# A new written order for the first half of a two-block attention kernel: 761 letters of TensorE work and 96 projections

## The chip, the cores and the metric

One core of one Trainium2 chip. The metric is the device time of one execution in microseconds (us), the median of several runs; less is better.

## What is computed

Two blocks of multi-head attention on their own inputs, their results side by side. Both have 2048 tokens, width 512 and 32 heads of 16. Block A looks back over a window of 256 tokens, block B at every token.

```python
qkv = (x @ wqkv).reshape(B, S, 3, H, Dh)          # both blocks, then q, k, v per head
scores = einsum("bhqd,bhkd->bhqk", q, k) * (Dh ** -0.5)
...
mask = (idx[:, None] - idx[None, :] >= 0) & (idx[:, None] - idx[None, :] < W)   # block A alone, W = 256
scores = where(mask, scores, -1e9)
...
p = softmax(scores)
out = einsum("bhqk,bhkd->bhqd", p, v) ... @ wo
return concatenate([a, b], axis=-1)
```

## The kernel before, in words

The program has two parts, one after the other on TensorE (PE). The first part does all of block A but its last projection, and also the projections to q, k and v of block B. The second part does block B by short cyclic patterns (line 45 on) and the output projections. The change touches the first part only.

The heads are in groups of four (g = 0 to 7), the queries in chunks of 512 (c = 0 to 3). A group and a chunk make a **unit**; each block has 32. Products of q, k and v go through HBM: a projection's result is copied out of PSUM, stored (`parts`, `vd`), and read back as the tiles `oq` (queries of one unit, 4 buffers), `opk` (keys of one group, 2 buffers) and `vt` (values).

The order of TensorE's work in the first part is written out by hand as a string, `ORDER_A`, one letter to a step:

- `p`: one projection on the whole array, 12 matmuls of 128 rows (line 309). Which one it is, the list `ORDER_P` says (`Aq02` is block A, queries, head pair 0, chunk 2; `Av13` is values, chunk 1, tile 3).
- `g`: a quarter of two projections that run side by side on two halves of the array's rows (line 444, 12 matmuls). Four `g` make two entries of `ORDER_P`.
- `m`: scores of one pair of heads for their maximum (line 607 for block A, line 561 for block B's first units); VectorE masks and reduces them (lines 616 and 617, or 612 and 564). It takes two neighbouring PSUM banks. Line 607's matmuls also use two halves of the rows. `e` is the same for block B's very first unit.
- `t`: the maxima of a unit are transposed (line 681), copied by ScalarE (683) and sent to the query tile by DMA (688).
- `s`: the scores again, of two heads, with the maximum as extra rows (line 717, two halves of the rows, two banks), then the exponential on ScalarE (line 724) and the mask on GpSimd (line 735).
- `w`: the exponentials times the values (line 764, matmuls on 32 columns of the array).

In the text below a projection is `p` or `g`, a maximum `m`, a score `s`, a weighing `w`, a transposition `t`. They use the array in three shapes: whole (`p`), halves of the rows (`g`, `m`, `e`, `s`) and columns (`w`, `t`).

While the program is being written, a planner (`Model`, line 90) keeps a clock for every engine and goes through the string (line 1122). It decides where between the letters DMAs are issued and copies are placed, and which PSUM banks a step gets; line 95 holds its charges for a change of shape. Loads of queries stand in a list of their own and come when the unit three before has its scores done:

```python
self.mode, self.turn = "f", dict(f=210, h=200, c=139)                 # line 95
...
list_("q", lambda u=u: done["s"] >= u - 3, stored(b, g // 2, 0, (c,)), load_q_at, b, g, c)   # line 1088
...
x = "p" if gen[0] else todo_a[0]                                      # line 1130
```

All DMAs are issued by SyncE's queue (SP), in one order. Everything is in order on its engine.

Of the kernel before, what the change touches and what calls it, by code (L numbers as in the profile page):

```python
# [57 lines left out]
FILL = 16  # L58
WARM = 22
ORDER_P = (  # L60
# [4 lines left out]
    "Bq20 Bq12 Bk30 Bk31 Bk10 Bq33 Bq30 Bq31 Bk32 Bq32 Bk33 Bk21 ").split()  # L65
WAKE = 200
GAP_V = 1500
PIECE = 4
# [4 lines left out]


ORDER_A = (
    "pppppppppppmmmmpmmgmgmptmgmgmmpmsgmsgmmpmsgmsgmwtsmgmsgmmpmsgsmgmtwwmmmpsmgmsgmswwmsgmsgmmpmssptwsmg"
    "msgmswsmgsmgmmwwmgmsgmstwmsgmsgmmwtsgmsgmswmsgmsgmswmmmpssmtwwmspmsmwssmgsmgmswtmsgsmgmwsmswssmwmmmp"
    "mtmswmsswmsmpsmmpsmwtmmmpsmswmmspmsmwsmsmwwtmsmsmsmpmsmtwsmsmwsmmswssmwmmspmmswsmwtsmgmsgmswsmgsmtgm"
    "mwsmwsmmswsmsmpsmmwmswtmsmwsmmmpmsssmmwsmsmwtmmmpsmswmsmsmwtsmsmwsmmpmmswsmtwmmmpmsgmsgmswtsmgmswpsm"
    "gsmwwmsgmmgmpmsgmsgsmwwtsmgmsgmswsmgsmgmmwtsgsmgsmwwmsgmsgmgsmgmswsmgmmgmwsmwtmsgmsgmswtmsgsmgmswwsm"  # L80
    "gmsgmswsmgsmgsmtwwmmmpmsmpmsmwsmmswtmsgmsgmswsmgsmgsmwmsmtwsmmswssmwmmmpmssmtwswmmmpmsgsmgsmwwmsgsmg"
    "etwmmmpmsgmsgmswsegsmgegesgmswsmgesgemtwmmpmsmwmswmsgsmgestwmsgesgmmpemmpmsmwwtemmpsmgmsgsmwmgegsewm"
    "mmpesstwmgmsgeswsmgsmgsmwesgsmgsmwmgsmgmswesmpsmmwtwmmmpmmmwp")
LAND = 400
LAND_V = 0
LGAP = 2500
# [1296 lines left out]
```

## Time and profile before

| | before |
|---|---|
| runs: median (lowest to highest) of 3 | 1776.33 us (1774.88 to 1779.42) |
| the profiled execution's own time | 1775.89 us |
| its span, first to last instruction | 1774.2 us |
| PE busy | 1756.8 us, 99% of the span |
| VectorE (DVE) busy | 1527.2 us, 86% |
| ScalarE (ACT) busy | 1402.2 us, 79% |
| GpSimd (POOL) busy | 648.5 us, 37% |
| granted TensorE clock | 1.000 of full speed |

The profile is of one execution. The time of an engine's instructions against the span is its share; PE's matmuls overlap and their ends are modelled, so that 99% does not say that PE never waits. The difference of the starts of two steps that follow each other on PE says what the first of them cost, its waiting and the wait of the next one included.

### The profile page before, as it was taken

To read this page: it belongs to the slowest core of one execution; us is meant where nothing else is said; L and a number is where in the kernel's file an instruction comes from. 1 tells how busy PE (TensorE), PEld (TensorE's weight loads), DVE (VectorE), ACT (ScalarE), POOL (GpSimd) and SP (SyncE) were. 2 spreads that over 40 slices of the span, in tenths; PEclk is the share of its full clock that TensorE was granted. 3 is DMA by queue.
4 is the path that set the end of the run, shared out by engine and by line. 5 is a ranking of instruction groups with operands and counts; after the bars stand their busy time and mean duration, and the time that the engine had idled before them with its cause. 6 is when DMAs were issued, how large, how long until landed. Compare 5 with 4: busy or idle time off the path is not lost.

```text
span 1774.2 us, 38875 instructions
## 1 busy us (share of the span) xinstructions
PE 1756.8 (99%) x14774; PEld 912.2 (51%) x14774; DVE 1527.2 (86%) x2386; ACT 1402.2 (79%) x2749; POOL 648.5 (37%) x1334
## 2 busy tenths in 40 slices
PE   8999999999999999999999999999999999999999
PEld 6776657767754444444444444444444444444456
DVE  4766786676779999999999999999999999999921
ACT  4466676665569888888889999999999999899894
POOL 0377888655755441222201123231112322121420
PEclk9999999999999999999999999999999999999999
DMA  8865667645663224111310311120031131010012
GB/s 267 200 210 199 206 206 223 177 146 163 201 181 108 66 86 89 41 41 41 83 37 17 77 29 30 47 62 17 17 78 35 30 65 38 17 38 26 20 44 102
DMA packets 129354, 166.78 MB, mean 94 GB/s; under 512 B 23204, under 2 KB 59044, under 8 KB 129156
## 3 DMA queue, kind: packets, MB, share of 16 engines
q1 hardware_dynamic: 129168, 164.31, 31.8%
q8 instruction: 116, 1.90, 0.5%
q14 instruction: 70, 0.57, 0.1%
HBM read 94.49 MB, written 68.19 MB: 92 GB/s over the span
## 4 chain that ended last, share of the span: by engine, by line
PE 89%; DVE 4%; DMA 2%; ACT 1%; SPq 1%; issue 1%; POOL 1%; POOLq 0%; ACTq 0%; DVEq 0%
PE ps_all L749 28%; PE ps_all L717 19%; PE ps_all L561 18%; PE ps_all L444 11%; PE ps_all L309 6%; PE ps_all L764 4%; DVE mt L564 3%; PE ps_all L607 3%; ACT p L724 1%; DMA in<-xT_A 1%; DVE nm L617 1%; PE ps_all L681 0%; SPq L473 0%; DVE ps_all L616 0%; DMA parts<-st 0%
## 5 line engine op out<-in xcount | busy, mean ns | idle before, releaser
L724 ACT ACTIVATE p<-ps_all 128x512 f32<-128x512 f32 x2432 | 1262.9, 598 | 204.8 <-PE ps_all L717 137.6
L564 DVE TENSOR_REDUCE mt<-ps_all 128x1 f32<-128x512 f32 (+1 forms) x1658 | 1212.7, 808 | 33.1 <-PE ps_all L561 28.0
L717 PE MATMUL ps_all<-oq,opk 51*128 51x512 f32 (+2 forms) x2752 | 756.9, 401 | 4.0 <-ACT p L724 2.0
L561 PE MATMUL ps_all<-opk,oq 48*128 48x512 f32 x2016 | 661.2, 435 | 0.2
L749 PE MATMUL ps_all<-p,vt 128*17 128x512 f32 (+1 forms) x5488 | 571.0, 490 | 0.0
L717 PEld LDWEIGHTS ps_all<-oq,opk 51*128 51x128 f32 x2752 | 385.8, 185 | 219.2 <-ACT p L724 142.7
L561 PEld LDWEIGHTS ps_all<-opk,oq 48*128 48x128 f32 x2016 | 304.6, 184 | 273.4 <-DVE mt L564 164.7
L735 POOL TENSOR_SCALAR_AFFINE_SELECT p<-p 128x256 f32<-128x256 f32 x480 | 179.0, 408 | 110.0 <-ACT p L724 107.4
L749 PEld LDWEIGHTS ps_all<-p,vt 128*17 128x17 f32 x5488 | 93.6, 95 | 214.2 <-issue 201.4
L616 DVE COPY_PREDICATED ps_all<-mone,ps_all 128x256 f32<-128x256 uint16 x224 | 95.3, 425 | 82.6 <-PE ps_all L607 75.9
L617 DVE TENSOR_REDUCE nm<-ps_all 128x2 f32<-128x512 f32 x224 | 155.2, 693 | 7.7
L633 POOL TENSOR_TENSOR mu<-mt 128x16 f32<-128x16 f32 x31 | 6.9, 222 | 409.9 <-DVE mt L564 409.9
L635 POOL TENSOR_TENSOR mu<-mt,mm 128x16 f32<-128x16 f32 x62 | 13.6, 220 | 388.7 <-DVE mt L564 388.7
L444 PE MATMUL ps_all<-x,w 64*128 64x512 f32 x720 | 119.2, 392 | 0.0
L444 PE MATMUL ps_all<-w_o,x_o 64*128 64x512 f32 x576 | 110.2, 394 | 0.0
L309 PE MATMUL ps_all<-x,w 128*128 128x512 f32 x408 | 102.7, 400 | 2.4 <-ACT x L257 1.7
L764 PE MATMUL ps_all<-p,vt 128*17 128x384 f32 (+2 forms) x1408 | 94.1, 386 | 0.1
L607 PE MATMUL ps_all<-opk,oq 48*128 48x384 f32 (+2 forms) x512 | 92.1, 361 | 2.0 <-DMA oq<-parts 0.5
L803 POOL TENSOR_TENSOR rd<-ld,minus 128x32 f32<-128x32 f32 x15 | 81.9, 5459 | 19.6 <-DMA ld<-od 19.6
L444 PEld LDWEIGHTS ps_all<-x,w 64*128 64x128 f32 x720 | 84.4, 185 | 8.9
L309 PEld LDWEIGHTS ps_all<-x,w 128*128 128x128 f32 x408 | 74.2, 188 | 24.8 <-ACT p L724 2.9
L392 ACT ACTIVATE raw<-ps_all 128x512 f32<-128x512 f32 x56 | 32.2, 596 | 68.5 <-PE ps_all L309 53.6
(79 smaller groups left out, 1042.7 us busy)
## 6 DMA issues: line engine op xcount, KB each, us to landing
parts<-st SPq DMA_DIRECT2D x64, 512.0 KB
oq<-parts SPq DMA_DIRECT2D x128, 128.0 KB
opk<-parts SPq DMA_DIRECT2D x128, 128.0 KB
od<-ou SPq DMA_DIRECT2D x64, 256.0 KB
vd<-vst SPq DMA_DIRECT2D x32, 272.0 KB
oq<-parts SPq DMA_DIRECT2D x128, 64.0 KB
opk<-parts SPq DMA_DIRECT2D x128, 64.0 KB
t<-od SPq DMA_DIRECT2D x32, 256.0 KB
```

The costliest lines, as they stand in the source:

```text
L309: nc.tensor.matmul(ps, l(u), r(v), start=start and k == 0, stop=stop and k == n - 1)
L444: op = nc.tensor.matmul(ps[a ^ turn], l(u)[rows], r(v)[rows], start=turn == q == 0, stop=turn == 1 and q == 11)
L561: nc.tensor.matmul(ps[:, a - lo], q[rows, 128 * qt:128 * qt + 128], k[rows, kc * QC:kc * QC + QC], start=True, stop=True)
L564: op = nc.vector.tensor_reduce(out=m[:, kc, lo:lo + len(sides), r, qt], in_=ps, axis=AX.X, op=ALU.max)
L607: nc.tensor.matmul(two[:, a, 0:w], opq[b, g, c][rows, r, 128 * qt:128 * qt + 128], opk2(g)[rows, r, t0:t1], start=True, stop=True)
L616: nc.vector.copy_predicated(two[:, :, 256:384], later, two[:, :, 0:128])
L617: op = nc.vector.tensor_reduce(out=m[:, :, r, qt, 0], in_=two[:, :, 128:384], axis=AX.X, op=ALU.max)
L717: nc.tensor.matmul(ps[x][:, col:col + n1], opk2(g)[rows, pr, 128 * k:128 * k + 128], opq[b, g, c][rows, pr, q0:q0 + n1], start=True, stop= ...
L724: op = nc.scalar.activation(p[:, a0 + x, :w], ps[x][:, :w], AF.Exp, scale=SCALE)
L735: nc.gpsimd.affine_select(out=v, in_=v, pattern=[[0, 2], [sign, 128]], compare_op=ALU.is_ge, fill=zero_fill, base=base, channel_multiplier ...
L749: nc.tensor.matmul(o[32 * j:32 * j + VW, q0:q1], vt[(g // 2) % 2][:, kt, vc:vc + VW], pts[1, g, c, kt, j // 2][:, j % 2, q0:q1], start=kt ...
L764: nc.tensor.matmul(o[32 * j:32 * j + VW, q0:q0 + w], vt[(g // 2) % 2][:, kt, vc:vc + VW], pts[b, g, c, m, j // 2][:, j % 2, col:col + w], ...
```

## The change

Only the two tables are new. The letters are the same in number (48 `p`, 96 `g`, 280 `m`, 16 `e`, 33 `t`, 192 `s`, 96 `w`), and so are the 96 entries of `ORDER_P`; their order is another from the fourth entry and the eleventh letter on. The planner's code and its charges stay as they were, and the second part of the program stays instruction by instruction.

```diff
 ORDER_P = (
-    "Aq00 Ak00 Ak01 Av11 Av02 Av03 Aq01 Av01 Ak02 Av21 Av13 Aq02 Av12 Av00 Aq03 Ak03 Av20 Av10 Av33 Ak20 Av32 "
...
+    "Aq00 Ak00 Ak01 Av03 Av02 Av11 Aq01 Aq02 Av00 Av23 Av10 Ak02 Av13 Av01 Aq03 Ak03 Av33 Av21 Av30 Av31 Ak10 "
...
 ORDER_A = (
-    "pppppppppppmmmmpmmgmgmptmgmgmmpmsgmsgmmpmsgmsgmwtsmgmsgmmpmsgsmgmtwwmmmpsmgmsgmswwmsgmsgmmpmssptwsmg"
...
-    "mtmswmsswmsmpsmmpsmwtmmmpsmswmmspmsmwsmsmwwtmsmsmsmpmsmtwsmsmwsmmswssmwmmspmmswsmwtsmgmsgmswsmgsmtgm"
...
+    "ppppppppppmmpmmpmmggmmpmgtmgmmpmsgmsgmmpmsgmsgmtwmmgsgmmpmsgmsgmtswwmmmpmsgssgswmsgmmptwmsgmmpsmswsm"
...
+    "ptmswmsswmmmpmmsptmsmwmmmpmsswmmspmsmwtsmsmwmsmswsmmpmtmswmswsmsmmswmmswssmmpmsmwwtmsgmsgsswmgsmgmst"
...
```

Counted over the whole strings, neighbours change like this (before, after): `s` then `m` 94, 37; `m` then `s` 97, 131; `s` then `g` 46, 72; `s` then `w` 32, 54; `w` then `m` 32, 55; `w` then `s` 31, 21; `m` then `w` 37, 17; `m` then `m` 59, 69; `m` then `g` 46, 18; `g` then `m` 59, 75. Changes of the array's shape (before, after): rows to columns 84, 92; columns to rows 84, 96; rows to whole 35, 38; whole to rows 35, 34; whole to columns 2, 4; columns to whole 2, 0. In sum 242 and 264.

Three places of which the prediction speaks. The first is ScalarE's queue in the first 45 us. `st` and `vst` are copies of projections out of PSUM (queries and keys; values), `x_3` is the splitting of the input's last chunk.

```order
 L388 ACTIVATE st_0_0_1_321<-ps_all 128x512
-L508 ACTIVATE vst_80<-ps_all 128x32x16
+L388 ACTIVATE st_0_0_2_337<-ps_all 128x512
 L257 ACTIVATE x_3_0_343<-in_3_0_288 128x512
 L257 ACTIVATE x_3_1_346<-in_3_0_288 128x512
-L257 ACTIVATE x_3_2_357<-in_3_2_290 128x512
-L257 ACTIVATE x_3_3_360<-in_3_2_290 128x512
-L388 ACTIVATE st_0_1_2_363<-ps_all 128x512
+L257 ACTIVATE x_3_2_358<-in_3_2_290 128x512
+L257 ACTIVATE x_3_3_361<-in_3_2_290 128x512
+L508 ACTIVATE vst_80<-ps_all 128x32x16
```

Before, the copy of the keys of chunk 2 (`st_0_1_2`) is the first thing after the splitting, and that of a value tile stands ahead of it; now the copy of the queries of chunk 2 (`st_0_0_2`) stands ahead of it, and the value tile's behind.

The second place is PE at the first use of the queries of unit (3,0), that is group 3, chunk 0 (`oq_3_0`), before:

```order
L717 MATMUL ps_all<-oq_2_1_1854,opk_75 128x256 x4
L607 MATMUL ps_all<-opk_75,oq_2_3_2210 128x384 x2
L717 MATMUL ps_all<-oq_2_1_1854,opk_75 128x384 x2
L717 MATMUL ps_all<-oq_2_1_1854,opk_75 128x128 x2
L607 MATMUL ps_all<-opk_75,oq_2_3_2210 128x384 x2
L309 MATMUL ps_all<-x_2_0_239,w_3_0_1298 128x512 x3
L309 MATMUL ps_all<-x_2_1_242,w_3_0_1298 128x512 x3
L309 MATMUL ps_all<-x_2_2_252,w_3_0_1298 128x512 x3
L309 MATMUL ps_all<-x_2_3_255,w_3_0_1298 128x512 x3
L607 MATMUL ps_all<-opk_76,oq_3_0_2450 128x128 x2
```

and now:

```order
L717 MATMUL ps_all<-oq_2_1_1991,opk_75 128x256 x4
L764 MATMUL ps_all<-p_2_0_2_0_2415,vt_78 17x256 x2
L764 MATMUL ps_all<-p_2_0_2_1_2448,vt_78 17x256 x2
L717 MATMUL ps_all<-oq_2_1_1991,opk_75 128x384 x2
L717 MATMUL ps_all<-oq_2_1_1991,opk_75 128x128 x2
L607 MATMUL ps_all<-opk_75,oq_2_3_2192 128x384 x2
L607 MATMUL ps_all<-opk_76,oq_3_0_2453 128x128 x2
L309 MATMUL ps_all<-x_1_0_168,w_3_0_1276 128x512 x3
L309 MATMUL ps_all<-x_1_1_171,w_3_0_1276 128x512 x3
L309 MATMUL ps_all<-x_1_2_189,w_3_0_1276 128x512 x3
L309 MATMUL ps_all<-x_1_3_192,w_3_0_1276 128x512 x3
```

A whole projection stood ahead of the first use of `oq_3_0` and now stands behind it. Between the last score that reads the buffer before (`oq_2_0`) and this first use there were 17 letters, `mwsmsmwwtmsmsmsmp`; now there are 15, `mwtsmsmwmsmswsm`. For unit (3,1) the letters between were `mtwsmsmwsmmswssmwm`, and are `wmswsmsmmswm`.

The third place is SP's queue ahead of the load of the same tile, before:

```order
L782 DMA od_0_3_1614<-ou_1_3_2391 128x512
L525 DMA vt_77<-vd_261 128x4x136
L411 DMA parts_2_1_935<-st_2_1_1_2294 128x2x512
L525 DMA vt_77<-vd_261 128x4x136 x2
L272 DMA in_1_0_2435<-xT_B 128x512
L796 DMA ld_0_3_2441<-od_0_3_1614 128x1x32
L489 DMA oq_3_0_2450<-parts_1_0_1411 16x2x512
```

and now:

```order
L782 DMA od_0_3_1617<-ou_1_3_2396 128x512
L525 DMA vt_77<-vd_261 128x4x136 x3
L796 DMA ld_0_3_2443<-od_0_3_1617 128x1x32
L411 DMA parts_2_1_2093<-st_2_1_2_2367 128x2x512
L489 DMA oq_3_0_2453<-parts_1_0_1164 16x2x512
```

The load of a piece of block B's input (`in_1_0`) no longer stands ahead of it; a store of keys (`parts_2_1`) now comes just before.

## Rows read from the trace of the kernel before

**Rows 1.** The page's first line: the span.

```profile
span 1774.2 us, 38875 instructions
```

**Rows 2.** Busy time by stretch: us, then each engine's, granted clock, DMA share, GB/s.

```profile
175.00:275.00 100.00, 95.36 (x869) 60.54 (x869) 77.67 (x186) 70.24 (x143) 85.64 (x161) 1.00 0.68 205
516.00:1748.00 1232.00, 1229.39 (x10158) 534.62 (x10156) 1164.68 (x1619) 1093.24 (x2135) 318.47 (x690) 1.00 0.19 50
```

**Rows 3.** PE in order of time, 508 to 520 us: start, us, what.

```profile
516.05 1.92 PE L1294 MATMUL ps_all<-mone 128*128 128x256 bf16 x16
```

**Rows 4.** PE in order of time, 108 to 117 us.

```profile
110.66 0.36 PE L607 MATMUL ps_all<-opk,oq 48*128 48x384 f32 x2
110.83 1.57 PE L444 MATMUL ps_all<-x,w 64*128 64x512 f32 x12
...
114.53 1.92 PE L764 MATMUL ps_all<-p,vt 128*17 128x256 f32 x32
116.38 0.44 PE L607 MATMUL ps_all<-opk,oq 48*128 48x384 f32 x2
```

**Rows 5.** PE in order of time, 139 to 150 us.

```profile
146.41 0.44 PE L607 MATMUL ps_all<-opk,oq 48*128 48x384 f32 x2
146.69 0.40 PE L717 MATMUL ps_all<-oq,opk 51*128 51x256 f32 x4
146.93 0.34 PE L607 MATMUL ps_all<-opk,oq 48*128 48x384 f32 x2
147.19 1.06 PE L764 MATMUL ps_all<-p,vt 128*17 128x128 f32 x16
148.18 0.80 PE L717 MATMUL ps_all<-oq,opk 51*128 51x384 f32 x8
149.24 0.45 PE L607 MATMUL ps_all<-opk,oq 48*128 48x384 f32 x2 [0.26 <-DVE nm L617]
```

**Rows 6.** Waits of PE's weight loads, 60 to 516 us: total us, times, longest.

```profile
PEld ps_all L717 <- ACT p L724: 12.2, 27, 0.9
...
PEld ps_all L607 <- ACT p L724: 5.6, 16, 0.6
```

**Rows 7.** PE in order of time, 26 to 46 us.

```profile
30.44 2.88 PE L309 MATMUL ps_all<-x,w 128*128 128x512 f32 x12
33.16 2.88 PE L309 MATMUL ps_all<-w_v,x 128*128 128x512 f32 x12
37.25 3.01 PE L309 MATMUL ps_all<-w_v,x 128*128 128x512 f32 x12 [1.21 <-DVE st L399]
40.19 0.60 PE L607 MATMUL ps_all<-opk,oq 48*128 48x128 f32 x5
...
41.78 3.02 PE L309 MATMUL ps_all<-x,w 128*128 128x512 f32 x12
```

**Rows 8.** ScalarE in order of time, 33 to 37 us.

```profile
33.38 2.41 ACT L257 ACTIVATE x<-in 128x512 fp32r<-128x512 f32 x4 [1.17 <-DMA in<-xT_A]
35.69 0.58 ACT L388 ACTIVATE st<-ps_all 128x512 fp32r<-128x512 f32 x1
```

**Rows 9.** PE in order of time, 186 to 203 us.

```profile
189.87 0.28 PE L717 MATMUL ps_all<-oq,opk 51*128 51x256 f32 x2
...
200.56 0.48 PE L607 MATMUL ps_all<-opk,oq 48*128 48x128 f32 x2
```

**Rows 10.** SP's queue in order of time, 188 to 216 us.

```profile
190.13 1.43 SPq L525 DMA_DIRECT2D vt<-vd  x2
...
193.55 2.87 SPq L489 DMA_DIRECT2D oq<-parts  x4
```

**Rows 11.** SP's queue in order of time, 394 to 418 us.

```profile
412.36 1.77 SPq L489 DMA_DIRECT2D oq<-parts  x4
```

**Rows 12.** PE in order of time, 413 to 418 us.

```profile
416.27 0.41 PE L607 MATMUL ps_all<-opk,oq 48*128 48x384 f32 x1 [0.24 <-DMA oq<-parts]
```

**Rows 13.** Waits of PE's weight loads, 180 to 280 us.

```profile
PEld ps_all L717 <- ACT p L724: 6.5, 14, 0.9
```

More of the change, by code (lines that the diff above doesn't have):

```diff
@@ L60 @@
 ORDER_P = (
[4 rows of a table removed]
-    "Bq20 Bq12 Bk30 Bk31 Bk10 Bq33 Bq30 Bq31 Bk32 Bq32 Bk33 Bk21 ").split()
[4 rows of a table added]
+    "Bq11 Bq23 Bk32 Bk31 Bq32 Bq33 Bk20 Bq31 Bk33 Bq12 Bk30 Bq30").split()
 WAKE = 200
@@ L75 @@
 ORDER_A = (
-    "pppppppppppmmmmpmmgmgmptmgmgmmpmsgmsgmmpmsgmsgmwtsmgmsgmmpmsgsmgmtwwmmmpsmgmsgmswwmsgmsgmmpmssptwsmg"
-    "msgmswsmgsmgmmwwmgmsgmstwmsgmsgmmwtsgmsgmswmsgmsgmswmmmpssmtwwmspmsmwssmgsmgmswtmsgsmgmwsmswssmwmmmp"
-    "mtmswmsswmsmpsmmpsmwtmmmpsmswmmspmsmwsmsmwwtmsmsmsmpmsmtwsmsmwsmmswssmwmmspmmswsmwtsmgmsgmswsmgsmtgm"
[L79 to L83, printed above, removed]
+    "ppppppppppmmpmmpmmggmmpmgtmgmmpmsgmsgmmpmsgmsgmtwmmgsgmmpmsgmsgmtswwmmmpmsgssgswmsgmmptwmsgmmpsmswsm"
+    "gmmgswmsgmsgmmwtsgmmgswmsgmsgmmwstwmsgmsgmswmsgmsgmmwsmpmsmtwswmmspmmswsgmsgmswtmsgmgmmswsmswsmswmms"
+    "ptmswmsswmmmpmmsptmsmwmmmpmsswmmspmsmwtsmsmwmsmswsmmpmtmswmswsmsmmswmmswssmmpmsmwwtmsgmsgsswmgsmgmst"
+    "wmswmmssswmmmpsmswmsmwmssmwtmmmpmsmwsmsmsmstmwmmpsmswmsmwsmsmsmtmwsmmpmswtmmswmmpmsgmsgmswmsgmsptwms"
+    "gmswwmsgmsgmmpmsgmsgmmtwwmgmmgswmsgmsgmswmsgmsgmswtmsgmsgmwtmsgmsgswmsgmgmswmmswsgmsgmswmsgmsgmmtwws"
+    "gmsgmswmsgmsgmmpmsmwtsmswmmmpmswsmswmsgmsgmtswmsgmsgmmtwmsmswmmmpmsswmmsmstwmswsswmmpmsgsegmtwwmsgms"
+    "gsewemmpesgmmgswmsgmsgmgmsgmswsegsegmmtwmmpmmswsmwtesgmsgmswmsgmsgmmpemmpmsmwtwemmpmsgmsgsewmgmsgmtw"
+    "seswmmmpsegemgswmsgsegmswmsgmsgsewsgmgeswmmspmswmmmpmmmtwwmmp")
 LAND = 400
```

6 rows, old and new, of the table ORDER_P are left out of this document.

## The prediction

> **What bounds the kernel now.** I read the span first, then busy time by stretch, then the order of time on TensorE (PE), then who waited for whom. The span is 1774.2 us [rows 1], and the first part, which alone is written anew, ends at 516.05, where line 1294 begins [rows 3]. From there to 1748 VectorE is busy for 1164.68 of 1232 us [rows 2], with instructions that the change leaves in place. So a gain or a loss is made in the first 516 us and carried unchanged to the end; the second part neither hides it nor adds to it. In the first part PE does nearly all of the waiting that counts: in its densest stretch, 175 to 275, PE is busy for 95.36 of 100 us, GpSimd for 85.64, VectorE for 77.67, ScalarE for 70.24 [rows 2]. No other engine is full there. What PE loses it loses in pieces of a few tenths, to PSUM banks that come free late, to queries that land late, and to changes of the array's shape. The clock is granted in full [rows 2], so it plays no part.
>
> The work itself is the same: as many letters of each kind, the same matmuls. I therefore price neighbours, places and transfers.
>
> **Changes of shape.** 264 instead of 242. The prices come from starts on PE. A maximum ahead of a projection quarter takes 110.83 - 110.66 = 0.17 us [rows 4], ahead of a weighing 147.19 - 146.93 = 0.26 [rows 5]: 0.09 for rows to columns. Two weighings in a row and then a maximum take 116.38 - 114.53 = 1.85 [rows 4], one and then a score 148.18 - 147.19 = 0.99 [rows 5]; the other is 0.86, so columns to rows is 0.13. A whole projection ahead of another takes 33.16 - 30.44 = 2.72, ahead of a maximum 40.19 - 37.25 = 2.94 [rows 7]: 0.22 for whole to rows. No row has rows to whole or whole to columns alone; I take the nearest, 0.09 and 0.22. With the counts: 8 x 0.09 + 12 x 0.13 + 3 x 0.09 - 1 x 0.22 + 2 x 0.22 - 2 x 0.13 = **+2.5 us**. PE pays this directly, nothing hides it. The rows show a price of 0.1 to 0.2 us for each change, and none between the different steps on halves of the rows. The Trainium skill, TensorEngine Tiling (Array Packing), section Tiling Modes, says that changing the tiling mode, and not just the tile, drains the engine; by that rule the change would only cost, and alone it would make the kernel 2.5 us slower, which is what the sum has before the waits are counted.
>
> **Neighbours that wait.** Maxima wait 5.6 us for exponentials, scores 12.2 us [rows 6], since a step can only start when an exponential has left its bank. A maximum straight behind a score takes over banks while ScalarE still works on the step before: 0.24 where it doesn't wait (146.69 to 146.93 [rows 5]). The 94 such pairs fall to 37. Put on these pairs, the 5.6 are 0.06 each, 57 fewer are -3.4. Against it, 34 more scores come straight behind a maximum; a score's mean wait for exponentials is 12.2 / 192 = 0.06, and I charge half of that, +1.0. Sum **-2.4 us**. Bounds: all 5.6 [rows 6] vanish, -5.6; or the waits only move to the next step and the 1.0 stays, +1.0. I take the middle since scores are now mostly followed by steps that take no pair of banks (72 and 54 times a quarter or a weighing, 46 and 32 before).
>
> **The start.** Before, the eleventh projection starts at 37.25 instead of 33.16 + 2.72 = 35.88: 1.37 lost, to a bank that VectorE frees late [rows 7]. It is late because ScalarE first splits the input's last chunk, 33.38 for 2.41, and copies the projection only from 35.69 [rows 8]. Then four maxima take 41.78 - 40.19 = 1.59 [rows 7] where 0.15 each would be 0.6: 1.0 lost. Now two maxima stand there, then a projection, then two more, so VectorE has the 2.9 us of the projection for the first two. But the first maximum gets the banks of the eighth and ninth projection, and the copy of the ninth (`vst_80`) is now behind the splitting: 33.38 + 2.41 + 0.58 = 36.4, so that the maximum starts at some 36.6 instead of 35.9, 0.7 lost. Sum **-1.7 us**, between -2.4 (nothing lost) and 0 (the same lost elsewhere).
>
> **Queries that land late.** A unit's queries are loaded when the scores that read the buffer before are done. Before, that score started at 189.87 and the first use was at 200.56 [rows 9], 10.7 us later; SP was busy from 190.13 with other loads and issued the four DMAs at 193.55 in 2.87 us [rows 10]. In a place where PE did wait, the four were issued from 412.36 in 1.77 [rows 11] and PE went on at 416.27 [rows 12]: 2.1 from the last issue's end to use. So 0.3 + 1.8 + 2.1 = 4.2 us are needed with SP free, 0.3 + 3.4 + 2.9 + 2.1 = 8.7 with SP as it was. The change takes the projection from between: the 15 letters left are, by the prices above, about 4.8 us (score 0.24, maximum 0.17 or 0.26, sixteen weighing matmuls 0.87, eight about half), and for unit (3,1) about 5.3. So PE may wait 0 to 3.9 and 0 to 3.4. One of the loads ahead of it on SP is gone, and PE's own waits stretch the interval; I take **+1.5 us** for both, bounds 0 and 7.3. On the other side, the wait of 0.24 at 416.27 [rows 12] and a like one 15 us earlier fall away, as the work between grows by some 3 and 5 us: **-0.5 us**, bounds -0.5 and 0.
>
> **Sum.** 2.5 - 2.4 - 1.7 + 1.5 - 0.5 = -0.6 us against the profiled execution's own 1775.89, so 1775.3. That execution lies 0.4 below the median of the runs, 1776.33; for a median I forecast 1775.7: no change. About 0.3%, 5.3 us, is what a measurement of this kernel can tell from no change. The ends of the terms together give -6.5 and +12.
>
> **Rivals.**
>
> Faster: the dense stretch opens. Of the 12.2 us that scores wait for exponentials, 6.5 are between 180 and 280 [rows 13]. Counted in the letters of that stretch, scores followed by a maximum fall from 35 to 23, with more weighings between. If ScalarE keeps up because its work comes evenly, half of all waits for exponentials go [rows 6], (12.2 + 5.6) / 2 = 8.9, instead of the 2.4 above: 1769.2, and to 1767 with the start at its best. For it: no engine is full [rows 2], so the waits are matters of order. Against it: GpSimd has 85.64 of 100 us there [rows 2] and must mask every exponential before it is weighed, and more maxima stand directly behind each other (69 for 59).
>
> Slower: queries become the wait. It takes the place of the bank waits where projections moved from ahead of a first use to behind it. Units (3,0) and (3,1) are followed by (4,2) and (5,2), with about 6.2 and 6.7 us of work between. If SP lags as it did [rows 10], 8.7 us are needed: 3.9 + 3.4 + 2.5 + 2.0 = 11.8, of which other waits that PE would have had anyway, some 4, are to be taken off. Instead of +1.5 that is +7.8: 1782. It decides from a lag of SP of about 0.6 us (4.8 - 4.2) for the first place; over 2 us for all four it is slower by more than 0.3%. For it: SP had such a lag at just this place. Against it: the first use came [rows 9, 10] 4.1 us after the last issue's end, without a wait.
>
> Nothing as meant: the letters are new, but line 95 keeps its charges, so that DMAs and banks are still placed by the planner's clock, which charges 0.14 to 0.21 for a change that costs 0.09 to 0.22 on PE [rows 4, 5, 7]. Where the planner's clock sets the waits, a new order wins and loses alike: 1776.3.
>
> **Chances.** Forecast 0.35; nothing as meant 0.07, also no change; faster 0.33; slower 0.25. So faster 0.33, same 0.42, slower 0.25. The range reaches past both rivals' times, 1767 and 1782, by about 2 us for terms that are not at their middle: 1765 to 1784; beyond it I leave one in ten on either side.
>
> **What would show it.** Line 1294 starts at 516.05 now; its new start minus this is the whole effect, whatever the sum. Right: it lies within 3 us; the eleventh step starts near 36.6; maxima wait less for exponentials than 5.6, and score waits stay near 12. The waits for queries appear at line 607 as waits for a DMA into `oq` near 190 to 215. Wrong: line 1294 starts before 511 with the dense stretch's 6.5 halved (the first rival), or after 521 with PE idle for DMAs into `oq` (the second), or the second part's length differs by more than 1 us, which would refute that it only carries the difference on.

## The result and the profile after

| | before | changed |
|---|---|---|
| median of 8 runs each (lowest to highest) | 1776.36 us (1774.88 to 1779.42) | 1782.24 us (1779.19 to 1786.82) |
| the profiled execution's own time, and its span | 1775.89, 1774.2 | 1782.23, 1780.5 |
| start of line 1294, the end of the first part | 516.05 | 521.77 |
| mean granted TensorE clock | 0.998 (72 later executions; 1.000 in the profiled one) | 0.997 (these 8 runs, and the profiled one) |

The ratio is 1.0035, with a 95% interval of 1.0024 to 1.0046: the new order is slower by about 6 us, a third of a per cent, where no change was forecast. The time lies inside the range of 1765 to 1784, but by luck: the range was drawn past the time of a rival, 1782, whose mechanism did not come.

The changed kernel's busy time by stretch (columns as in [rows 2]):

```profile
175.00:275.00 100.00, 94.75 (x816) 59.84 (x814) 74.42 (x179) 67.00 (x137) 81.45 (x155) 0.97 0.64 197
521.80:1754.00 1232.20, 1229.57 (x10157) 534.51 (x10156) 1164.64 (x1619) 1092.87 (x2135) 319.22 (x691) 1.00 0.19 49
```

In the second part VectorE is busy for 1164.64 us, as before (1164.68 [rows 2]). In the dense stretch fewer matmuls are done in the same 100 us (816 for 869), and the granted clock, the third column from the end, is 0.97 instead of 1.00. Finer stretches show where:

```profile
250.00:254.00 4.00, 2.29 (x26) 1.23 (x18) 2.72 (x15) 3.57 (x7) 3.44 (x6) 1.00 0.68 212
...
256.00:262.00 6.00, 6.00 (x30) 3.90 (x23) 3.66 (x9) 1.66 (x4) 4.85 (x9) 0.53 0.52 173
262.00:266.00 4.00, 4.00 (x50) 2.38 (x52) 1.98 (x4) 3.13 (x7) 1.46 (x5) 1.00 0.25 76
526.00:528.00 2.00, 1.88 (x11) 0.98 (x14) 2.00 (x4) 1.98 (x5) 0.00 (x0) 0.96 1.07 169
528.00:531.00 3.00, 3.00 (x18) 0.92 (x14) 2.19 (x3) 1.29 (x4) 0.00 (x0) 0.50 1.06 179
```

From 254.8 to 261.6 us, and again from 527.9 to 531.3, TensorE runs at half its clock, 1.2 instead of 2.4 GHz. The profile of before has no such stretch. PE in order of time shows what it did ahead of the first:

```profile
250.27 0.56 PE L717 MATMUL ps_all<-oq,opk 51*128 51x128 f32 x4
250.66 0.28 PE L607 MATMUL ps_all<-opk,oq 48*128 48x256 f32 x2
251.59 0.56 PE L717 MATMUL ps_all<-oq,opk 51*128 51x128 f32 x4 [0.65 <-ACT p L724]
251.98 0.28 PE L607 MATMUL ps_all<-opk,oq 48*128 48x256 f32 x2
252.91 0.50 PE L717 MATMUL ps_all<-oq,opk 51*128 51x256 f32 x4 [0.65 <-ACT p L724]
253.25 0.34 PE L607 MATMUL ps_all<-opk,oq 48*128 48x384 f32 x2
254.18 0.50 PE L717 MATMUL ps_all<-oq,opk 51*128 51x256 f32 x4 [0.59 <-ACT p L724]
...
258.16 4.16 PE L309 MATMUL ps_all<-x,w 128*128 128x512 f32 x10
```

Scores and maxima alternate, each score waits 0.6 us for an exponential, and PE is busy for 2.29 of 4 us. Then ten matmuls of a projection take 4.16 us, where twelve take 3.01 at full clock [rows 7]. The Trainium skill, TensorE: Matmul & The Clock Gate, section "A second HAM failure mode: psum-queue depth-cycling", tells of another kernel whose PE idles a little between groups of matmuls as it goes round its PSUM banks and loses clock by it. At 250 us the trace fits that. Ahead of the second fall PE was busy for 1.88 of 2 us (526 to 528), so there the rule explains nothing. Nor does such idling always bring a fall: the profile of before has this stretch, at full clock throughout.

```profile
202.00:206.00 4.00, 2.62 (x32) 1.48 (x28) 1.68 (x10) 2.22 (x6) 3.92 (x7) 1.00 0.82 266
```

The waits of PE's weight loads in the changed first part, 60 to 521 us (total us, times, longest):

```profile
PEld ps_all L607 <- ACT p L724: 10.3, 24, 1.0
PEld ps_all L717 <- ACT p L724: 9.5, 17, 1.0
PEld ps_all L607 <- DVE nm L617: 6.8, 16, 0.7
```

Scores wait less for exponentials (9.5 for 12.2 us), maxima nearly twice as long (10.3 for 5.6) [rows 6].

### The profile page after: what moved, and what is told of

It reads as the page before. It is cut to its first block, busy times and chain, and to the rows that moved or that the text cites. A ratio compares the mean times of both kernels' runs of the same rounds, so it can differ in the third digit from the quotient of the medians.

```text
span 1780.5 us, 38856 instructions
## 1 busy us (share of the span) xinstructions
PE 1762.9 (99%) x14774; PEld 912.9 (51%) x14774; DVE 1526.5 (86%) x2386; ACT 1401.8 (79%) x2749; POOL 648.7 (36%) x1334
## 4 chain that ended last, share of the span: by engine, by line
PE 92%; DVE 4%; POOL 1%; ACT 1%; DMA 1%; issue 1%; SPq 0%; POOLq 0%; ACTq 0%; DVEq 0%
PE ps_all L749 28%; PE ps_all L561 18%; PE ps_all L717 18%; PE ps_all L444 11%; PE ps_all L309 9%; PE ps_all L764 4%; PE ps_all L607 3%; DVE mt L564 3%; ACT p L724 1%; PE ps_all L681 1%; DVE nm L617 0%; DMA in<-xT_A 0%; DVE ps_all L616 0%; DMA oq<-parts 0%; SPq L489 0%
## 5 line engine op out<-in xcount | busy, mean ns | idle before, releaser
L564 DVE TENSOR_REDUCE mt<-ps_all 128x1 f32<-128x512 f32 (+1 forms) x1658 | 1212.4, 806 | 34.2 <-PE ps_all L561 28.5
L444 PE MATMUL ps_all<-x,w 64*128 64x512 f32 x720 | 125.0, 391 | 0.0
L444 PE MATMUL ps_all<-w_v,x 64*128 64x512 f32 x432 | 87.8, 393 | 0.0
```

The source lines that it names most:

```text
L444: op = nc.tensor.matmul(ps[a ^ turn], l(u)[rows], r(v)[rows], start=turn == q == 0, stop=turn == 1 and q == 11)
L564: op = nc.vector.tensor_reduce(out=m[:, kc, lo:lo + len(sides), r, qt], in_=ps, axis=AX.X, op=ALU.max)
```

## Experiments

`B` and `C` are the strings of before and of the change, `Bp` and `Cp` their projection lists; `C[334:348]` are the letters 335 to 348. Fourteen kernels, before among them, differ in order alone, or nearly so. A straight line of time against mean granted clock, with one slope for all 184 executions and a level for each kernel, gives 1.47 us for each 0.001 of clock; slopes of their own fit the kernels no better. That parts an order's own time (the level at full clock) from what the clock takes. The difference of a level from that of before has a standard error of 0.3 to 0.5 us, so that levels less than about 0.8 us apart are hardly told apart. One slope is also a simplification: in the profiles of before and of the change, the fall behind line 1294, 3.4 us at half clock and so 1.7 us of lost clock, lengthens the second part by only 0.6. The ratio is to runs of before taken beside each kernel.

| kernel | median us | ratio to before [95%] | mean clock | at full clock, over before |
|---|---|---|---|---|
| before (72 runs) | 1777.03 | 1 | 0.9982 | 0 (1775.0) |
| change | 1782.24 | 1.0035 [1.0024, 1.0046] | 0.9970 | +3.2 |
| change, letters 335 to 348 given back | 1780.70 | 1.0020 [1.0011, 1.0029] | 0.9983 | +3.8 |
| before with these letters of the change | 1779.15 | 1.0014 [1.0004, 1.0024] | 0.9973 | +0.8 |
| change, seven maxima twice | 1782.83 | 1.0031 [1.0018, 1.0045] | 0.9970 | +4.4 |
| before up to 300, then change | 1785.43 | 1.0038 [1.0025, 1.0052] | 0.9951 | +2.6 |
| change, four stretches given back | 1781.61 | 1.0024 [1.0014, 1.0033] | 0.9983 | +4.6 |
| before with four stretches of the change | 1785.20 | 1.0047 [1.0034, 1.0061] | 0.9984 | +8.6 |
| change with before's tail | 1784.10 | 1.0039 [1.0025, 1.0052] | 0.9964 | +4.1 |
| before with the change's tail | 1776.92 | 0.9997 [0.9987, 1.0007] | 0.9989 | +0.7 |
| change up to 348, then before | 1785.59 | 1.0041 [1.0029, 1.0053] | 0.9972 | +5.9 |
| before up to 348, then change | 1780.73 | 1.0019 [1.0010, 1.0027] | 0.9964 | +0.2 |
| change, letters 422 to 586 given back | 1783.13 | 1.0034 [1.0022, 1.0045] | 0.9971 | +4.3 |
| before with letters 422 to 586 of the change | 1778.08 | 1.0000 [0.9988, 1.0012] | 0.9989 | +1.5 |

**The fourteen letters ahead of the fall.** Given back in the change, put alone into before, and left in place with seven of their maxima's matmuls issued twice, so that PE idles less between them.

```diff
-ORDER_A = C                                        # mwsmsmsmstmwmm
+ORDER_A = C[:334] + B[334:348] + C[348:]           # ssmmwsmsmwtmmm
```

> The changed kernel with 14 of its 761 letters (the 335th to the 348th, mwsmsmsmstmwmm) put back to those of the kernel before (ssmmwsmsmwtmmm). Clock theory (these letters leave TensorE waiting for exponentials so long that its granted clock falls to 1.2 GHz for 6.8 us, 3.4 us lost): clock 1.000 from 240 to 300 us, line 1294 at about 517 to 518.5, time about 1778. Rival (the loss is many small waits all over the new order, the clock only goes along): these 14 letters give back 1 us at most, line 1294 at 521, time 1781.

```diff
-ORDER_A = B
+ORDER_A = B[:334] + C[334:348] + B[348:]
```

> The kernel before with the same 14 letters put in from the change. Clock theory: the granted clock falls to 1.2 GHz a little after 254 us for some 5 to 8 us, line 1294 at 519 to 521, time 1779 to 1781. Rival (many small waits): 1 us more than before, 1777.5, clock 1.000.

```diff
-        for a in range(2):
+        for a in [0, 1] * (2 if 129 <= nm < 136 else 1):
```

> The changed kernel, and the seven maxima among those 14 letters have their matmuls issued twice, with the same result: some 0.17 us more TensorE work for each while it would wait for exponentials anyway, no wait taken away. Clock theory: with TensorE busier in that stretch the clock holds or falls for less time, time 1777 to 1780 in spite of the added work. Rival (waits and work, not the clock): 0 to 1.2 us slower than the change, 1782 to 1783.5.

The letters do bring waits and a fall: in before they take 9.4 us instead of 6.7, with half clock from 253.9 to 260.7. Given back, they take 7.0 and the fall at 254.8 is gone. But the profile then has another, behind another place where PE idles:

```profile
196.00:200.00 4.00, 3.18 (x34) 1.56 (x26) 3.37 (x7) 3.05 (x8) 3.92 (x10) 1.00 0.75 164
201.00:207.00 6.00, 6.00 (x15) 4.18 (x15) 1.17 (x8) 0.36 (x2) 1.12 (x3) 0.50 0.46 158
254.00:262.00 8.00, 6.74 (x70) 3.99 (x67) 5.85 (x24) 7.50 (x15) 6.77 (x14) 1.00 0.46 150
```

The kernel gains 1.5 us in the median, which is not clear of noise; the clock alone, 0.9983 for 0.9970, is worth 1.9. At full clock nothing is won. So the clock theory's 1778 did not come; the rival's 1781 did. Put alone into before, the letters brought the fall and the time that the clock theory gave (1779.15), of which 0.8 us is left at full clock. The fall near 200 does not belong to the change's letters alone: two kernels with before's letters there, before up to 348, then change, and before with letters 422 to 586 of the change, fell at 197 to 199, where the profile of before did not. Whether a fall comes at such a place differs from one execution to the next.

Matmuls issued twice kept no clock: half clock still came, from 257.7, 271.4 and 530.8, and the time is the rival's. But they did not fill the idle time either: the scores still waited for exponentials, and in the 4 us ahead of the first fall PE was busy for 2.53, hardly more than the 2.29 of the change. Whether filled idle time would hold the clock is therefore not shown.

```profile
253.00:257.00 4.00, 2.53 (x28) 1.67 (x24) 2.68 (x12) 3.38 (x7) 3.92 (x7) 1.00 0.58 180
```

**A cut at 300.** There the two orders have done the same letters and the same projections.

```diff
-ORDER_A, ORDER_P = C, Cp
+ORDER_A, ORDER_P = B[:300] + C[300:], Bp[:46] + Cp[46:]
```

> The first 300 letters and 46 projections of the kernel before, the rest of the change. Clock theory: the 14 letters are in the part kept from the change, so the loss stays: clock falls near 254 us, time 1780 to 1782. Rival (small waits all over): about half of the loss goes, 1779.

Both expectations missed: the time is 1785.43. The first 300 letters given back win 0.6 us at full clock, no more than noise, and the clock is the lowest of all, 0.9951. That seemed to put the loss behind letter 300; the cut at 348 below contradicts it.

**Stretches by their price in the two profiles.** Giving back the four dearest of the change; taking over its four cheapest.

```diff
-ORDER_A = C
+ORDER_A = C[:199] + B[199:224] + C[224:334] + B[334:348] + C[348:421] + B[421:586] + C[586:725] + B[725:]
```

> The changed kernel with the letters 200 to 224, 335 to 348, 422 to 586 and 726 to 761 given back from before; ORDER_P stays the changed one. In the profiles these four stretches took 1.4, 2.4, 1.8 and 0.4 us more than before, and the letters behind the second took 2.0 more while the granted clock was at half. Theory 'stretches add up': a stretch keeps its price in the other order, so line 1294 starts at 521.8 - 8.0 = 513.8, about 2 us earlier than in the kernel before, and the time is about 1774.0. Rival 'the price is not the stretch's own' (banks and DMA places are set anew by the planner, and the waits come up elsewhere): less than half comes back, line 1294 starts at 518 or later, 1778 or more.

```diff
-ORDER_A = B
+ORDER_A = B[:33] + C[33:74] + B[74:253] + C[253:300] + B[300:383] + C[383:421] + B[421:586] + C[586:650] + B[650:]
```

> The kernel before with the letters 34 to 74, 254 to 300, 384 to 421 and 587 to 650 of the change; ORDER_P stays that of before. In the profiles these stretches took 0.3, 0.9, 0.3 and 1.0 us less in the changed kernel. 'Stretches add up': line 1294 starts at 516.05 - 2.5 = 513.6, the time is about 1773.9. Rival 'the price is not the stretch's own': line 1294 starts at 516 or later, 1776.4 or more.

Both fell clearly to the rival: line 1294 starts at 523.0 and 525.2, where 513.8 and 513.6 were expected. Time of the same stretch in several profiles, from starts on PE:

| letters | before | change | change, four given back | before, four taken | before, 422 to 586 of change |
|---|---|---|---|---|---|
| 75 to 115 | 27.8 | 28.4 | 28.4 | 27.8 | 27.8 |
| 200 to 224 | 17.2 | 18.6 | 18.2 | 17.2 | 17.2 |
| 335 to 348 | 6.7 | 9.1 | 7.0 | 8.4 | 6.7 |
| 422 to 480 | 34.2 | 34.6 | 34.3 | 34.2 | 35.7 |
| 554 to 586 | 18.7 | 19.2 | 20.0 | 18.7 | 19.3 |
| 587 to 650 | 41.9 | 40.9 | 41.7 | 46.2 | 40.5 |

Where letters and surroundings are the same, a stretch repeats: letters 75 to 115 take 27.8 us in all seven profiles with before's letters there, 28.4 in all seven with the change's. Moved between other letters and another projection list, it doesn't keep its price: 25 letters of before keep 1.0 of the change's 1.4 us, and the 1.0 that letters 587 to 650 seemed to win belongs to the stretch ahead of them: before's own letters take 40.5 behind the change's 422 to 586. The 46.2 has a cause of its own: behind the older projection list the first scores of block B come too early for their keys, which takes 2.1 us, and 3.4 us at half clock follow, from 409.4. The 0.9 us that letters 254 to 300 seemed to win were chance: before's own letters take 27.7 us there in its profile and 26.3 in four of the five others.

```profile
407.89 0.46 PE L561 MATMUL ps_all<-vt,qe 48*128 48x512 f32 x1 [1.51 <-DMA vt<-parts]
408.99 0.47 PE L561 MATMUL ps_all<-vt,qe 48*128 48x512 f32 x1 [0.63 <-DMA vt<-parts]
```

**The tail, for the second fall.** The last 36 letters exchanged, each way.

```diff
-ORDER_A = C
+ORDER_A = C[:725] + B[725:]
```

> The changed kernel with its last 36 letters given back from before. Theory 'the tail lets the clock fall': the stretch at half clock 6 us behind line 1294's start is gone, the second part takes 1258.1 us as before instead of 1258.7, the mean granted clock over the runs rises by about 0.001, and with the 0.4 us of the tail itself the time is about 1780.5. Rival 'the fall comes from what follows, not from the tail': a stretch at half clock remains within 15 us of line 1294, and the time is 1782.

```diff
-ORDER_A = B
+ORDER_A = B[:725] + C[725:]
```

> The kernel before with the last 36 letters of the change. Theory 'the tail lets the clock fall': a stretch of 3 to 10 us at half clock appears some 6 us behind line 1294's start, the second part takes 1258.7 us or more, the time is 1777.5 to 1779. Rival 'the fall comes from what follows': the clock stays in full, the second part takes 1258.1, and the time is 1776.5 to 1777.

The tail is cleared: half clock comes at 528 to 531 with before's tail, and does not come with the change's tail in before, which is as fast as before.

**A clean cut at 348.** Each half of the change alone.

```diff
-ORDER_A, ORDER_P = C, Cp
+ORDER_A, ORDER_P = C[:348] + B[348:], Cp[:48] + Bp[48:]
```

> The first 348 letters and 48 projections of the change, the rest of before; both orders have done the same letters and the same projections at this cut. 'Stretches add up where the cut is clean': the stretches up to here took 3.9 us more than before by the profiles, and 1.5 more went to the letters just behind while the granted clock was at half: line 1294 starts at 516.05 + 3.9 to 5.4 = 520 to 521.5, no stretch at half clock near 528, the second part takes 1258.1, the time is about 1781, 4 us over before. Rival 'even at a clean cut the price is not the stretch's own': letters 349 to 761, which are those of before, take over 1 us more than the 256.5 us that they took there (at full clock), or the time differs by more than 2 us from 1781.

```diff
-ORDER_A, ORDER_P = C, Cp
+ORDER_A, ORDER_P = B[:348] + C[348:], Bp[:48] + Cp[48:]
```

> The first 348 letters and 48 projections of before, the rest of the change. 'Stretches add up where the cut is clean': behind the cut the change took 0.3 less, 1.8 more, 1.0 less and 0.4 more: line 1294 starts at 516.05 + 0.9 = 517.0; with a stretch at half clock near 528 (0.6 us) the time is about 1778.5, 1.5 us over before. The excess of this run over before and that of the run with the first 348 letters add to the 5.9 of the change within 1.5 us. Rival: they do not, or the letters up to 348, which are those of before, take over 1 us more than there.

The levels are +5.9 and +0.2. The first holds a wait that neither parent has, behind the cut, for the splitting of a piece of block B's weights for the values, of which GpSimd does part:

```profile
303.57 0.49 PE L444 MATMUL ps_all<-w_v,x 64*128 64x512 f32 x1 [1.70 <-POOL w_v L258]
```

The letters 384 to 421 take 28.7 us there instead of 25.7. In medians the two missed their expectations by 4.6 and 2.2 us, and by the signs set beforehand both fell to their rivals: the letters behind the cut took 263.7 us for the 260.7 of before, and the two excesses, 8.8 and 4.0 in the medians, add to 12.8 and not to 5.9. Only afterwards, without these 3.0 us, of which the trace shows 1.7 as that wait, and at full clock, are the levels +2.9 and +0.2, with the sum 3.1 beside the change's 3.2. This agreement was not forecast. The second's profile, with before's letters up to 348:

```profile
198.00:201.00 3.00, 3.00 (x9) 2.33 (x8) 1.76 (x6) 1.08 (x2) 3.00 (x9) 0.50 0.98 322
266.00:272.00 6.00, 6.00 (x28) 4.03 (x21) 4.10 (x11) 3.07 (x6) 6.00 (x12) 0.50 0.43 153
526.00:528.00 2.00, 2.00 (x10) 0.15 (x8) 1.78 (x3) 1.03 (x2) 0.00 (x0) 0.50 1.01 116
```

So, as far as the levels go, the order's own loss lies in the first 348 letters: behind before's first 348 the change's letters cost nothing at full clock (+0.2), but clock (0.9964 in the mean). Against the cut at 300: between the two cuts stand only the change's letters 301 to 348, and at full clock they would cost 2.4 us there, but the fourteen of them cost 0.8 in before and win nothing when given back. The cost of these letters is not settled.

**Letters 422 to 586.** Exchanged alone, each way, since all profiles with the change's letters there had the fall near 528 and the others none.

```diff
-ORDER_A = C
+ORDER_A = C[:421] + B[421:586] + C[586:]
```

> The changed kernel with the letters 422 to 586 of before (ORDER_P of the change). Theory 'these letters bring the fall of the clock behind line 1294' (all five profiles with the change's letters there have a stretch at half clock at 527 to 541 us, the four without have none): none here, the second part takes 1258.1; the letters themselves 1.8 us less, at the seams some tenths more: time 1780 to 1781. Rival 'the fall there is chance, or another stretch's': a stretch at half clock at 525 to 540 remains.

```diff
-ORDER_A = B
+ORDER_A = B[:421] + C[421:586] + B[586:]
```

> The kernel before with the letters 422 to 586 of the change (ORDER_P of before). Theory 'these letters bring the fall of the clock behind line 1294': a stretch at half clock of 3 to 10 us some 6 us behind line 1294's start, the second part takes 1258.7 or more; the letters themselves 1.7 us more: time 1779.5. Rival 'chance, or another stretch's': full clock there, the second part takes 1258.1, time 1778.8 by the letters alone.

Without them the fall near 528 is gone, but in before they bring none. Six of six profiles with the change's letters 349 to 725 and its list have it, none of the eight others, before among them. No shorter piece was found to bring it. So they are needed for it, but not enough. Giving back the letters did not make the change faster (1783.13, where 1780 to 1781 was expected).

## Why the prediction was wrong

Two steps failed, the clock and the neighbours; the second is the larger.

**The clock:** "The clock is granted in full, so it plays no part." One profiled execution showed it so; over 72 executions of before the mean is 0.9982, and the change's is 0.9970. The difference times 1.47 is 1.8 us of the loss, with a standard error of some 0.7 from the scatter of the clock. In the profiled execution the fall at 254.8 is 6.8 us at half, a loss of 3.4 / 1776 = 0.0019 of clock, or by the slope an estimated 2.8 us.

**Neighbours**, "57 fewer are -3.4", sum -2.4. Maxima and scores together waited 17.8 us for exponentials [rows 6] and now wait 19.8: "the waits only move to the next step" is what came, and by more than the +1.0 that this bound allowed. Where they went shows when what each step takes beyond the shortest time of its kind (the lowest twentieth, by size and by the shape of the next step, over the fourteen profiles; steps at half clock left out) is added up by pairs. A score and then a maximum lost 9.7 us at 94 places and lose 6.5 at 37, so the -3.4 came nearly whole, though each place left became dearer, 0.18 us for 0.10. A maximum and then a score lost 8.9 and lose 11.6, +2.7 where +1.0 was charged. Two maxima in a row, 4.0 and now 5.5, and a score and then a weighing, 1.4 and now 3.1, stood in the sum at nothing. So the error is not the gain but the price of what took its place. PE in order of time in the new order, 169 to 176 us, shows one:

```profile
169.83 1.06 PE L764 MATMUL ps_all<-p,vt 128*17 128x128 f32 x16
170.82 0.62 PE L607 MATMUL ps_all<-opk,oq 48*128 48x384 f32 x4
171.83 0.44 PE L607 MATMUL ps_all<-opk,oq 48*128 48x384 f32 x2 [0.39 <-ACT p L724]
172.20 3.04 PE L309 MATMUL ps_all<-x,w 128*128 128x512 f32 x12
175.16 0.62 PE L607 MATMUL ps_all<-opk,oq 48*128 48x384 f32 x4
```

and the order before, 170 to 175 us:

```profile
170.26 1.06 PE L764 MATMUL ps_all<-p,vt 128*17 128x128 f32 x16
171.25 0.44 PE L607 MATMUL ps_all<-opk,oq 48*128 48x384 f32 x2
171.52 0.40 PE L717 MATMUL ps_all<-oq,opk 51*128 51x384 f32 x4
171.76 0.40 PE L607 MATMUL ps_all<-opk,oq 48*128 48x384 f32 x2
172.21 3.00 PE L309 MATMUL ps_all<-x,w 128*128 128x512 f32 x12
```

From the weighing to the projection it took 172.21 - 170.26 = 1.95 us, and takes 172.20 - 169.83 = 2.37: three maxima in a row, in place of a maximum, a score and a maximum, and the third waits for banks that an exponential still holds.

**Changes of shape** were right. The same shortest times, by the shape of the next step alone, give 0.09 for rows to columns, 0.13 for columns to rows, 0.21 for whole to rows, and 0.09 and 0.21 for the two changes that no row had: +2.4 us where 2.5 was predicted. If instead every pair of neighbouring steps is charged the short end (the lowest twentieth) of the differences of its starts in nine profiles, the first part's steps come to 459.3 us before and 461.2 now, +1.9. What is over, the waits, rose from 46.7 to 51.4 us, with the clock's 2.8 in it. Pairs 1.9, waits at full clock 1.9 and clock 2.8 are 6.6; the first projection started 0.9 earlier, the second part is 0.6 longer: 6.3, the difference of the two profiled executions. By the rule of the Trainium skill, TensorEngine Tiling (Array Packing), section Tiling Modes, a change of the tiling mode drains the engine; the traces agree in that every kind of change cost 0.09 us or more.

**The start**, -1.7, came as shown for the steps it named:

```profile
35.61 0.50 PE L607 MATMUL ps_all<-opk,oq 48*128 48x128 f32 x4
36.04 2.99 PE L309 MATMUL ps_all<-w_v,x 128*128 128x512 f32 x12
...
55.92 0.44 PE L607 MATMUL ps_all<-opk,oq 48*128 48x384 f32 x2
57.52 0.61 PE L717 MATMUL ps_all<-oq,opk 51*128 51x384 f32 x3 [1.15 <-issue]
```

The maximum starts at 35.61, even earlier than the 36.6 forecast, and the next projection at once. But a wait of 1.15 us is new at 57.52: "the same lost elsewhere", the bound of 0. The first 33 letters take 53.0 us in the mean of seven profiles with before's letters, 52.9 in seven with the change's, spread over 1.5 and 2.3 us. So of the -1.7 some 0.1 is seen.

**Queries**, +1.5 and -0.5: SP issued the four loads for unit (3,0) from 192.70 in 2.71 us, and the first use waits at 199.03 for 0.22; none is seen at the second place, and the wait at 416.27 [rows 12] is gone. So +0.2 and -0.5, inside the bounds, though from the last issue's end to use it took 3.6 us where 2.1 was reckoned.

```profile
192.70 2.71 SPq L489 DMA_DIRECT2D oq<-parts  x4
...
199.03 0.32 PE L607 MATMUL ps_all<-opk,oq 48*128 48x128 f32 x1 [0.22 <-DMA oq<-parts]
```

This rules out **the slower rival**: its time, 1782, came out, and "after 521", but not "with PE idle for DMAs into `oq`". **The faster rival** fell with the neighbours. **The second part** carried the difference on as said, but for 0.6 us at the fall near 528. The ends of the terms, as they are given, add to -6.0 and +10.8, not to -6.5 and +12; nothing hangs on it.

Not tried: another length of line 1294's run of matmuls, orders that keep PE's idle time the same while they change the neighbours, and other charges in line 95, so that "nothing as meant" was not tested beyond its time, 1776.3, which did not come. No version beat before clear of noise.

## What to carry to other kernels

When an order is written anew, charge what is structural (changes of shape) and expect waits on a full ring of buffers to move rather than vanish: a wait belongs to the stretch and what stands around it, not to a pair of letters, and a stretch that looks cheap in one order may owe that to the one ahead of it. Where a difference of 0.3% is at stake, one profile with full clock says little about the clock: part time and clock over many executions first.

## What was not expected of the hardware

- TensorE fell to half clock for 3 to 10 us inside a program that keeps PE at 99% of the span, at different places in different profiles, and 0.001 of mean clock goes with 1.47 us.
- PE's idle time alone does not explain these falls. Of 23 falls in twelve of the profiles (before, and before with the change's tail, have none), 13 came behind 4 us in which PE was busy for at most 3.3, such as the first below, 2.61 of 5 in before with four stretches taken over; ten came at 3.7 to 3.9 of 4, six of them near 528 and four at 265 to 271 (the third line, of the change with before's tail, whose clock fell at 269). Their cause stays open.

```profile
404.00:409.00 5.00, 2.61 (x19) 1.67 (x18) 1.55 (x5) 2.99 (x6) 2.67 (x7) 1.00 0.42 125
410.00:412.00 2.00, 2.00 (x14) 1.47 (x12) 0.72 (x1) 0.00 (x0) 0.00 (x0) 0.50 0.71 208
265.00:269.00 4.00, 3.71 (x34) 2.30 (x34) 3.86 (x8) 3.50 (x9) 3.92 (x9) 1.00 0.51 155
```

- Times of a stretch with the same letters and surroundings repeat within 0.1 us in most of the first part, but those of letters 254 to 300 come at 27.5 to 27.7 or at 26.3 for the same letters there, and the first 33 letters spread over some 2 us.
